# Attention, gated MLP and their gradients on one core: the first part's factors in pieces, its weights loaded inside the loop, the last gate sums in a row, and the gradients' loads moved

## The chip, the cores and the metric

The kernel runs on one core of a Trainium2 chip. A core has five engines that work side by side, each on its own list of instructions and strictly in the order of that list: TensorE (PE, matrix products; its weight loads are listed as PEld), VectorE (DVE), ScalarE (ACT), GpSimd (POOL) and SyncE (SP). Transfers between the chip's main memory and the core's two on-chip memories, SBUF and PSUM, are carried by 16 DMA engines; an engine's queue issues them. An instruction waits on semaphores until what it needs is there, and everything behind it on its engine waits with it.

The metric is the time of one execution on the device in microseconds (us). Where a time is given for a kernel, it is the median of its runs; a profile is one further execution, with a trace of every instruction.

## The reference, cut to what matters

```python
S, D, H, F = 2048, 512, 32, 1792           # Dh = 16

def _B_ref(x, w1, b1, w2, b2):
    y = _layernorm(x, axis=-1)
    h = _gelu(y @ w1 + b1)
    return h @ w2 + b2

def forward(x, wqkv, wo, w1, b1, w2, b2):
    xn = _layernorm(x, axis=-1)
    s = attention(xn, wqkv) @ wo           # 32 heads, softmax(q k / 4) v
    g = _silu(_B_ref(xn, w1, b1, w2, b2))
    return x + s * g

out, vjp = jax.vjp(forward, A_x, A_wqkv, A_wo, B_w1, B_b1, B_w2, B_b2)
return (out, *vjp(grad_out))
```

Inputs are bf16 (x and grad_out 1 x 2048 x 512). The outputs are the forward result and the gradients of x and of the six weights.

## The kernel before

The rows of x are cut into 16 tiles of 128 (`NT`), and four tiles make a group. The kernel writes its order out by hand: each engine gets its instructions in the order in which the Python code emits them, and no scheduler moves them. Nearly all transfers are issued on SP's queue (`ld = nc.sync.dma_start`, and `tr`, a transfer that transposes on its way).

There are three parts, one behind the other.

**First part** (class `Pre`, L102 to L482, up to about 220 us). At its start, x, wqkv, b1, b2, w1, the four transposed pieces of wo (`woT`, L160) and w2 are issued; POOL meanwhile clears the attention's operand 0 (`make_op`, L35, called for operand 0 at the start and for operand 1 near the end of this part): two memsets of 128 x 2048 (`KVT` L47, `QDT` L48) and two of one row (L50).

The loop over row tiles `t` (L296 to L329) works ahead of itself. In iteration t, `stats(t + 6)` takes mean and variance on DVE (L180, L181). `t_xn(t + 1)` transposes the normalised rows on PE, and DVE copies them out (`tp`, L173 to L177: four transposes into PSUM, then one copy, on DVE where its last argument is 1, on ACT where it is 0). At t = 1, 5 and 9 `factors(t + 3, t + 7)` (L183) works out the two norm factors of four tiles: a root on ACT, a reciprocal and two products on DVE, a root on ACT, a reciprocal on DVE. `norm(t + 2)` scales the rows in place on DVE (L195). `norm2(t + 2)` writes the second norm's rows on ACT (L199) into `yr`, which has four slots, so that it must wait until the store of `Y_s` (L319, two tiles, issued on SP at odd t) has read the slot. Between these, `proj3` makes the three projections (L210), and their results are copied out and transposed (`t_kvq`) for the attention. At t = 2 `bias1` turns b1 into a column (L279). Whole groups are stored at t = 4, 8 and 12 (`squares`, `stores`).

Behind the loop, from about 92.5 us, comes the hidden layer and the gate. `hid(g, fc)` is a product with w1, gelu and two stores. `gate(t)` is a product with w2, then on DVE and ACT the gate's value, the product `dsr` with grad_out (L373 to L379, called the chain) and four more operations, `gate_b` (L385 to L388), which run on POOL for t below 13 and on DVE for 13, 14 and 15. `t_ds(t)` transposes `dsr` into `dsoT`, `dproj(t)` multiplies it by `woT` (L396) and copies it to `ndc` (L397), and `t_do(t)` transposes that into `dOT`. In the loop `dproj` runs two tiles and `t_do` three tiles behind `gate`; `dsoT` and `ndc` have two slots each. The last of them, and the last `gate_b`, stand behind the loop.

**Attention** with its own gradients (`attention_core`, L1051 to L1414, about 220 to 1843 us).

**Gradients** (class `Grads`, L490 to L1048, its end from 1843 us on). A first loop over t (`emit_so`, `emit_oT`, `emit_dmT`) finishes the forward result tile by tile; `emit_dwo` (L732), from t = 12, makes the gradient of wo from `dso_all`, which is loaded in two halves (L752, L767). Then a loop over the 14 column blocks `fc` of the hidden layer: `emit_dw2(fc)` (L742) takes one transposed block `hgr` (four slots; `load_hg`, L713, a transposing transfer), and `load_hg(fc + 4)` is issued behind it. In these loops SP also issues `load_h1(a, b)` (`gp`, L659, plain loads used much later), `xn1` in four quarters (L800, L810), and `load_dkv` (`dKVn`, L790, transposing). The next loop over i makes the gradient of wqkv: `emit_dwq` from `xn1`, then `emit_dwkv` (L827) from the two halves of `dKVn`, four products each.

## Time and profile before

| | |
|---|---|
| Runs of the kernel (median, smallest, largest) | 2181.61, 2180.7, 2186.16 us |
| Profiled execution: time | 2180.46 us |
| Profiled execution: span of its trace | 2178.8 us |
| PE busy | 2133.0 us, 98% of the span |
| DVE busy | 1898.0 us, 87% |
| ACT busy | 1782.2 us, 82% |
| POOL busy | 870.6 us, 40% |
| Transfers | 461.17 MB, mean 212 GB/s |

A row of a timeline reads: start (us from the span's start), duration in us, engine, line of the kernel, operation, output <- inputs, how many follow each other; in brackets the idle time of the engine just before, and what ended it. Rows of engine SPq are SP's issues of transfers; their duration is the time that SP spent on them, not that of the transfer. A row of a line's own view begins with the line, and gives the durations in ns (smallest, median, largest) and the first and last start.

### The profile page before, as it was taken

The page shows a single profiled execution, that of the slowest core. Times are in us where ns is not written, and L with a number is a line of the kernel's source. Part 1 is how long each engine was busy: PE and PEld are TensorE (multiplying, and loading weights), DVE is VectorE, ACT ScalarE, POOL GpSimd, SP SyncE. Part 2 cuts the span into 40 slices and gives each one's busy share as a digit, 9 for nine tenths or more (in the row PEclk, how much of TensorE's full clock was granted, in tenths as well). Part 3 has the DMA queues.
Part 4 walks back from the last instruction along what each step waited for, and adds up shares of the span by engine and source line. Part 5 has one row for each costly group of instructions (what it writes and reads, how often), then busy time and mean ns, then how long its engine had stood idle before and what let it go on. Part 6 is the DMA issues. An engine that isn't in the chain of part 4 may idle for free.

```text
span 2178.8 us, 74934 instructions
## 1 busy us (share of the span) xinstructions
PE 2133.0 (98%) x30659; PEld 1170.6 (54%) x30659; DVE 1898.0 (87%) x3523; ACT 1782.2 (82%) x2481; POOL 870.6 (40%) x2397
## 2 busy tenths in 40 slices
PE   6999999999999999999999999999999999899999
PEld 3444555555555555555555555555555555444444
DVE  6677899999999999999999999999999998788647
ACT  5664899999999999999999999999999997775224
POOL 4376434343434444343434344444434343511003
PEclk9999999999999999999999999999999999999999
DMA  7786999999999999999999999999999999999975
GB/s 235 248 281 202 205 199 198 209 195 200 208 204 198 209 201 201 202 200 206 203 199 201 202 203 201 204 203 204 200 202 206 194 213 212 294 251 240 246 209 178
DMA packets 1416569, 461.17 MB, mean 212 GB/s; under 512 B 1329118, under 2 KB 1400414, under 8 KB 1416224
## 3 DMA queue, kind: packets, MB, share of 16 engines
q1 hardware_dynamic: 1401920, 425.44, 100.3%
q0 software_dynamic: 12720, 29.37, 4.9%
q8 instruction: 240, 3.93, 0.8%
q10 hardware_dynamic: 1584, 1.57, 0.2%
q14 instruction: 105, 0.86, 0.1%
HBM read 62.79 MB, written 64.75 MB: 59 GB/s over the span
## 4 chain that ended last, share of the span: by engine, by line
PE 94%; DVE 2%; DMA 1%; ACT 1%; POOL 0%; issue 0%; SPq 0%; DVEq 0%; ACTq 0%; POOLq 0%
PE tT L1192 22%; PE Z L1334 15%; PE d L1137 15%; PE X L1239 6%; PE X L1232 5%; PE X L1235 5%; PE s L1115 3%; PE ps_dy L909 2%; PE ps_dw L742 2%; PE ps_dw L983 2%; PE ps_h L352 2%; PE ps_m L367 2%; PE ps_dh L875 2%; PE tT L1266 1%; PE ps_dxa L1027 1%; PE ps_dwkv L827 1%
## 5 line engine op out<-in xcount | busy, mean ns | idle before, releaser
L1155 DVE TENSOR_TENSOR gts<-d,ets 128x512 bf16<-128x512 f32 x2048 | 1302.2, 682 | 18.2 <-PE d L1137 3.9
L1124 ACT ACTIVATE ets<-s 128x1024 bf16<-128x1024 f32 x1024 | 1051.6, 1027 | 15.2 <-PE d L1137 3.9
L1208 ACT COPY ek<-tT 128x448 f32<-128x448 f32 (+1 forms) x1024 | 525.1, 513 | 115.0 <-PE tT L1192 31.3
L1192 PE MATMUL tT<-ident_bf,ets 128*128 128x128 bf16 x6790 | 557.9, 221 | 0.0
L1192 PEld LDWEIGHTS <-ets 128*128 128x128 bf16 x6790 | 382.5, 98 | 210.5 <-issue 195.2
L1137 PE MATMUL d<-QDT,KVT 32*128 32x512 bf16 x2048 | 469.4, 384 | 0.0
L1153 POOL COPY gts<-ets 128x128 bf16<-128x128 bf16 x1024 | 281.6, 297 | 387.5 <-ACT ets L1124 382.7
L1115 PE MATMUL s<-QDT,KVT 32*128 32x512 bf16 x2048 | 401.1, 379 | 2.4 <-ACT ets L1124 2.4
L1334 PE MATMUL Z<-gk,W 128*32 128x512 bf16 x2304 | 302.9, 389 | 1.4 <-DVE acc L1348 1.3
L1239 PE MATMUL X<-gts,NAT 128*17 128x256 bf16 x4096 | 290.6, 273 | 0.0
L1232 PE MATMUL X<-ets,NAT 128*32 128x256 bf16 x4096 | 290.4, 273 | 0.0
L1235 PE MATMUL X<-ets,Lc 128*32 128x256 bf16 x4096 | 290.3, 273 | 0.0
L1334 PEld LDWEIGHTS <-W 128*32 128x32 bf16 x4096 | 105.5, 93 | 238.2 <-issue 225.0
L1137 PEld LDWEIGHTS <-KVT 32*128 32x128 bf16 x2048 | 148.5, 91 | 114.3 <-issue 21.5
L1334 PE MATMUL Z<-ek,W 128*32 128x512 bf16 x1792 | 203.6, 389 | 0.0
L1235 PEld LDWEIGHTS <-Lc 128*32 128x32 bf16 x4096 | 110.1, 97 | 108.6
L1215 DVE COPY ek<-tT 128x64 f32<-128x64 f32 x378 | 84.9, 225 | 89.5 <-ACT ek L1208 76.0
L1404 POOL COPY tick<-gts 1x2 bf16<-1x2 bf16 x205 | 36.0, 175 | 313.5 <-DVE gts L1155 313.5
L1115 PEld LDWEIGHTS <-KVT 32*128 32x128 bf16 x2048 | 142.7, 91 | 12.3 <-issue 6.4
L1239 PEld LDWEIGHTS <-NAT 128*17 128x17 bf16 x4096 | 114.7, 91 | 15.4 <-issue 1.1
L1232 PEld LDWEIGHTS <-NAT 128*32 128x32 bf16 x4096 | 108.8, 96 | 5.1 <-issue 5.1
L1295 POOL TENSOR_TENSOR W<-NATQq,rL 128x128 bf16<-128x128 bf16 x64 | 25.5, 399 | 147.9 <-DVE rL L1294 110.3
(252 smaller groups left out, 2470.4 us busy)
## 6 DMA issues: line engine op xcount, KB each, us to landing
gk<-gts SPq DMA_TRANSPOSE x512, 5.6
H1T_s<-h1r SPq DMA_DIRECT2D x28, 256.0 KB, 4.2
HGT_s<-hgT SPq DMA_DIRECT2D x8, 896.0 KB, 4.5
DH_s<-stg SPq DMA_DIRECT2D x12, 512.0 KB, 3.3
hch<-DH_s SPq DMA_DIRECT2D x12, 512.0 KB, 4.8
gp<-H1T_s SPq DMA_DIRECT2D x9, 512.0 KB, 6.8
out_dram<-ob_w POOLq DMA_DIRECT2D x36, 128.0 KB, 4.6
NAT_s<-NS SPq DMA_DIRECT2D x4, 1056.0 KB, 6.1
```

What stands on the lines that cost most here:

```text
L1115: nc.tensor.matmul(s[:, hj, :], lhsT=op["KVT"][r:r + 32, kb * 128:(kb + 1) * 128], rhs=op["QDT"][r:r + 32, qc * 512:(qc + 1) * 512], start ...
L1124: nc.scalar.activation(out=st_et[g].rearrange("k b h q -> k h b q"), in_=cur["s"][:].rearrange("k h (b q) -> k h b q", b=4), func=ACT.Exp)
L1137: nc.tensor.matmul(d[:], lhsT=op["KVT"][r:r + 32, kb * 128:(kb + 1) * 128], rhs=op["QDT"][r:r + 32, qc * 512:(qc + 1) * 512], start=True, ...
L1153: nc.gpsimd.tensor_copy(out=gts[:, kb % 2, 8, :], in_=st_et[g][:, b // 2, b % 2, :])
L1155: nc.vector.tensor_tensor(out=gts[:, kb % 2, 4 * hj:4 * hj + 4, :], in0=st_d.pop((g, hj))[:].rearrange("k (b q) -> k b q", b=4), in1=st_et ...
L1192: nc.tensor.transpose(tb[:, i - cut(g), :], et[:, b // 2, b % 2, :], ident_bf[:])
L1208: nc.scalar.copy(out=blk[j]["Ek"][kb // 4][:, kb % 4, c:7].rearrange("q i k -> q (i k)").bitcast(f32), in_=st_T[g][:, 0:(7 - c) * 64])
L1215: nc.vector.tensor_copy(out=blk[g // 16]["Ek"][kk // 4][:, kk % 4, i].bitcast(f32), in_=st_T[g][:, 448:512])
L1232: nc.tensor.matmul(X[r:r + 32, 0:256], lhsT=NATt[:, kb, hj, 1:33], rhs=ev, start=(kb == 0), stop=False, skip_group_check=True, tile_positi ...
L1235: nc.tensor.matmul(X[r:r + 32, 256:512], lhsT=Lc[:], rhs=ev, start=False, stop=False, skip_group_check=True, tile_position=(0, r))
L1239: nc.tensor.matmul(X[r:r + 17, 256:512], lhsT=NATt[:, kb, hj, 0:17], rhs=gv, start=False, stop=(kb == 15), skip_group_check=True, tile_pos ...
L1334: nc.tensor.matmul(Z[r:r + 32, :], lhsT=WT[j % 2][1 - part][:, qb, hj, :], rhs=mv, start=(part == 0 and qb == 0), stop=(part == 1 and qb = ...
```

## The change

Seven things, in the order of the diff:

1. The memset of `QDT` of operand 0 is done by DVE; that of operand 1 stays on POOL.
2. w1 (two halves, t = 3 and 5), w2 (two halves, t = 7 and 9) and the transposes of wo (two each at t = 11 and 13) are issued by a new function `weights(t)` inside the loop, behind the store of `Y_s`; before, all of them were issued ahead of the loop.
3. `factors` can be called in four parts. In the loop part 0 (first root) stays at its old place, part 1 (reciprocal and two products) follows `t_y`, part 2 (second root) follows the third projection's call `proj3(t, 2)`, and part 3 (last reciprocal) comes after the last `t_kvq`. The second root has a row of its own to write to.
4. `bias1` is called at t = 9 rather than 2.
5. At the end of the gates, the sums of gates 13, 14 and 15 follow each other on PE with only `t_ds` between them; `dproj` from 11 and `t_do` from 10 on come behind the loop, interleaved. `dsoT` and `ndc` have four slots each, the former with the help of `xnT`, which is free by then. `gate_b(13)` runs on DVE between the chains of 13 and 14; `gate_b(14)` and `gate_b(15)` come last. `t_ds(14)` is emitted twice, in the loop at t = 15 and behind it.
6. Gradients, first loop: the second half of `dso_all` is loaded at t = 3 rather than 5; five loads of `gp` come at t = 5, 7, 9, 11 and 15, where seven came at t = 3, 5, 7 and 12 to 15.
7. Gradients, loop over fc: the quarters of `xn1` are loaded at fc = 4, 6, 8 and 10, where two came ahead of the loop and two at 9 and 11; `gp` is loaded at every odd fc, where it was at the even ones from 2 on. In the loop of the gradient of wqkv, `gp`'s fourth set is loaded at i = 0 to 3, one more than before.

```diff
@@ -45,7 +45,7 @@
         t["NATQq"] = pool.tile([128, 16, 2, 16], bf16, name="NATQq")
         t["NATQd"] = pool.tile([128, 16, 2, 16], bf16, name="NATQd")
     nc.gpsimd.memset(t["KVT"][:], 0.0)
-    nc.gpsimd.memset(t["QDT"][:], 0.0)
+    (nc.vector if i == 0 else nc.gpsimd).memset(t["QDT"][:], 0.0)
     for hj in range(2):
         nc.gpsimd.memset(t["KVT"][32 * hj:32 * hj + 1, :], -1.0)
     return t
@@ -155,10 +155,17 @@
         b1_bf = sm.tile([FC, 128], bf16, name="b1_bf")
         ld(out=b1_bf[:], in_=B_b1.rearrange("(c p) -> c p", p=128))
         ld(out=b2bc[:], in_=B_b2.rearrange("(o d) -> o d", o=1).to_broadcast([128, D]))
-        ld(out=w1_sb[:], in_=B_w1.rearrange("(c p) f -> p c f", p=128))
-        for ac in range(IC):
-            nc.sync.dma_start_transpose(out=woT[:, :, ac * 128:(ac + 1) * 128], in_=A_wo[ac * 128:(ac + 1) * 128, :])
-        ld(out=w2_sb[:], in_=B_w2.rearrange("(c p) d -> p c d", p=128))
+
+        def weights(t):
+            if t in (3, 5):
+                i = (t - 3) // 2
+                ld(out=w1_sb[:, 2 * i:2 * i + 2], in_=B_w1.rearrange("(c p) f -> p c f", p=128)[:, 2 * i:2 * i + 2])
+            if t in (7, 9):
+                i = (t - 7) // 2
+                ld(out=w2_sb[:, 7 * i:7 * i + 7], in_=B_w2.rearrange("(c p) d -> p c d", p=128)[:, 7 * i:7 * i + 7])
+            if t in (11, 13):
+                for ac in (t - 11, t - 10):
+                    nc.sync.dma_start_transpose(out=woT[:, :, ac * 128:(ac + 1) * 128], in_=A_wo[ac * 128:(ac + 1) * 128, :])
 
         nc.gpsimd.memset(Bsel[:], 1.0)
         nc.gpsimd.affine_select(out=Bsel[:], in_=Bsel[:], compare_op=ALU.is_ge, fill=0.0, base=0,
@@ -180,16 +187,21 @@
             nc.vector.bn_stats(out=st6[:, t, :], in_=xt[:, t, :])
             nc.vector.bn_aggr(out=mv[:, t, :], in_=st6[:, t, :])
 
-        def factors(t0, t1):
+        def factors(t0, t1, part=None):
             r1, r2 = k.rstd1[:, t0:t1], k.rstd2[:, t0:t1]
             v = mv[:, t0:t1, 1]
             a, b = lnv[:, 0, t0:t1], lnv[:, 1, t0:t1]
-            nc.scalar.activation(out=a, in_=v, func=ACT.Sqrt, bias=k.eps_t[:], scale=1.0)
-            nc.vector.reciprocal(out=r1, in_=a)
-            nc.vector.tensor_tensor(out=b, in0=v, in1=r1, op=ALU.mult)
-            nc.vector.tensor_tensor(out=b, in0=b, in1=r1, op=ALU.mult)
-            nc.scalar.activation(out=a, in_=b, func=ACT.Sqrt, bias=k.eps_t[:], scale=1.0)
-            nc.vector.reciprocal(out=r2, in_=a)
+            c = lnv[:, 2, t0:t1]
+            if part in (0, None):
+                nc.scalar.activation(out=a, in_=v, func=ACT.Sqrt, bias=k.eps_t[:], scale=1.0)
+            if part in (1, None):
+                nc.vector.reciprocal(out=r1, in_=a)
+                nc.vector.tensor_tensor(out=b, in0=v, in1=r1, op=ALU.mult)
+                nc.vector.tensor_tensor(out=b, in0=b, in1=r1, op=ALU.mult)
+            if part in (2, None):
+                nc.scalar.activation(out=c, in_=b, func=ACT.Sqrt, bias=k.eps_t[:], scale=1.0)
+            if part in (3, None):
+                nc.vector.reciprocal(out=r2, in_=c)
 
         def norm(t):
             nc.vector.tensor_scalar(out=xt[:, t, :], in0=xt[:, t, :], scalar1=mv[:, t, 0:1], scalar2=k.rstd1[:, t:t + 1],
@@ -298,14 +310,16 @@
                 stats(t + 6)
             if t + 1 < NT:
                 t_xn(t + 1)
-            if t % 4 == 1 and t + 7 <= NT:
-                factors(t + 3, t + 7)
+            fac = (lambda part: factors(t + 3, t + 7, part)) if t % 4 == 1 and t + 7 <= NT else (lambda part: None)
+            fac(0)
             if t + 2 < NT:
                 norm(t + 2)
                 norm2(t + 2)
             proj3(t, 1)
             t_y(t)
+            fac(1)
             proj3(t, 2)
+            fac(2)
             if t >= 1:
                 t_kvq(t - 1, 1, 1)
                 t_kvq(t - 1, 2, 0)
@@ -313,11 +327,13 @@
             proj3(t, 0)
             if t >= 1:
                 t_kvq(t - 1, 0, 1)
+            fac(3)
             spread(t, 2)
             spread(t, 0)
             if t % 2 == 1:
                 ld(out=k.Y_s.rearrange("(t p) d -> p t d", p=128)[:, t - 1:t + 1], in_=yr[:, (t - 1) % 4:(t - 1) % 4 + 2, :])
-            if t == 2:
+            weights(t)
+            if t == 9:
                 bias1()
             if t % 4 == 0 and t >= 4:
                 squares(t // 4 - 1, 1)
@@ -341,8 +357,14 @@
         gd = mid.tile([128, 8, D], bf16, name="gd", tag="m4")
         gw, dsr = gd[:, 0:4, :], gd[:, 4:8, :]
         tau = mid.tile([128, D], f32, name="tau", tag="m6")
-        dsoT = mid.tile([128, 2, IC, 128], bf16, name="dsoT", tag="m5")
-        ndc = nat[:, :, 0, :]
+        dsoT2 = mid.tile([128, 2, IC, 128], bf16, name="dsoT", tag="m5")
+
+        def dsoT(t):
+            return (dsoT2, xnT)[t // 2 % 2][:, t % 2]
+
+        def ndc(t):
+            return nat[:, t % 2, t // 2 % 2, :]
+
         h1v = k.H1T_s.rearrange("(c p) s -> p c s", p=128)
         hgv = k.HGT_s.rearrange("(c p) s -> p c s", p=128)
 
@@ -377,7 +399,7 @@
                 nc.vector.tensor_scalar(out=sg, in0=ta, scalar1=0.5, scalar2=0.5, op0=ALU.mult, op1=ALU.add)
                 nc.vector.tensor_tensor(out=G_, in0=m_, in1=sg, op=ALU.mult)
                 nc.vector.tensor_tensor(out=dsr[:, t % 4, :], in0=dot, in1=G_, op=ALU.mult)
-            if t < NT - 1:
+            if t < 14:
                 chain()
             return chain, lambda e: gate_b(e, B_, G_, sg, dot)
 
@@ -388,18 +410,18 @@
             e.tensor_tensor(out=B_, in0=B_, in1=dot, op=ALU.mult)
 
         def t_ds(t):
-            tp(lambda b: dsr[:, t % 4, b * 128:(b + 1) * 128], dsoT[:, t % 2], 0)
+            tp(lambda b: dsr[:, t % 4, b * 128:(b + 1) * 128], dsoT(t), 0)
 
         def dproj(t):
             ps = psA.tile([128, 512], f32, name="ps_do", tag="mm")
             for bc in range(IC):
-                nc.tensor.matmul(ps[:], lhsT=dsoT[:, t % 2, bc, :], rhs=woT[:, bc, :], start=(bc == 0), stop=(bc == IC - 1))
-            nc.vector.tensor_copy(out=ndc[:, t % 2, :], in_=ps[:])
-            nc.gpsimd.tensor_copy(out=ND[:, (t // 4) % 2, :, t % 4, :], in_=ndc[:, t % 2, :].rearrange("p (a c) -> p a c", a=NPAIR))
+                nc.tensor.matmul(ps[:], lhsT=dsoT(t)[:, bc, :], rhs=woT[:, bc, :], start=(bc == 0), stop=(bc == IC - 1))
+            nc.vector.tensor_copy(out=ndc(t), in_=ps[:])
+            nc.gpsimd.tensor_copy(out=ND[:, (t // 4) % 2, :, t % 4, :], in_=ndc(t).rearrange("p (a c) -> p a c", a=NPAIR))
 
         def t_do(t):
             g = (t // 4) % 2
-            tp(lambda b: ndc[:, t % 2, b * 128:(b + 1) * 128], dOT[:, g, :, (t % 4) * 128:(t % 4) * 128 + 128], 0)
+            tp(lambda b: ndc(t)[:, b * 128:(b + 1) * 128], dOT[:, g, :, (t % 4) * 128:(t % 4) * 128 + 128], 0)
 
         def after(t, f=lambda: None):
             if t % 4 == 3:
@@ -423,7 +445,6 @@
         def load_dot(g):
             ld(out=dotr[:, g % 2], in_=go2[:, g * 4:g * 4 + 4])
 
-        lastb = []
         load_dot(0)
         for fc in range(FC):
             hid(0, fc)
@@ -445,22 +466,16 @@
                 gate_store(t - 1)
             if t == 0:
                 bound()
+            if t == 14:
+                continue
             chain, gb = gate(t)
             if t == 0:
                 stores_nat(3)
             if t < 13:
                 gb(nc.gpsimd)
-            else:
-                lastb.append(gb)
-            if t >= 2:
+            if t >= 2 and t < 13:
                 dproj(t - 2)
-            if t == 14:
-                lastb[0](nc.vector)
-                gate_store(13)
-            if t == NT - 1:
-                chain()
-                lastb[1](nc.vector)
-            if t >= 3:
+            if t >= 3 and t < 13:
                 t_do(t - 3)
                 after(t - 3)
             if t >= 1:
@@ -469,16 +484,32 @@
                 load_dot(g + 2)
             if 2 <= t < 6:
                 wkv_rows(t - 2)
-        t_do(NT - 3)
-        t_ds(NT - 1)
-        dso_store(NT - 1)
+            if t == 13:
+                chain14, gb14 = gate(14)
+                gb(nc.vector)
+                chain14()
+                t_ds(13)
+                gate_store(13)
 
         nc.scalar.activation(out=b2bc[0:1, 0:1], in_=b2bc[0:1, 0:1], func=ACT.Exp)
-        dproj(NT - 2)
-        dproj(NT - 1)
-        t_do(NT - 2)
-        t_do(NT - 1)
-        lastb[2](nc.vector)
+        dproj(11)
+        chain()
+        t_do(10)
+        t_ds(14)
+        dproj(12)
+        t_do(11)
+        after(11)
+        dproj(13)
+        t_ds(15)
+        dso_store(15)
+        t_do(12)
+        dproj(14)
+        t_do(13)
+        dproj(15)
+        t_do(14)
+        t_do(15)
+        gb14(nc.vector)
+        gb(nc.vector)
         after(NT - 1, lambda: gb_store(NT - 1))
 
 
@@ -761,19 +792,21 @@
                 nd += 1
             if t == 3:
                 self.load_s1(5)
-                load_h1(0, 0)
+                ld(out=dso_all[:, 8:16], in_=dsov[:, 8:16])
             if t == 5:
                 self.load_s1(6)
-                ld(out=dso_all[:, 8:16], in_=dsov[:, 8:16])
-                load_h1(0, 1)
+                load_h1(0, 0)
             if t == 7:
                 self.load_s1(7)
-                load_h1(0, 2)
+                load_h1(0, 1)
             if t in (8, 9, 10, 11):
                 load_hg(t - 8)
+            if t in (9, 11):
+                load_h1(0, (t - 5) // 2)
             if t >= 12:
                 emit_dwo(t - 12)
-                load_h1((t - 9) // 4, (t - 9) % 4)
+            if t == 15:
+                load_h1(1, 0)
         self.flush_adds()
         while nd < NT:
             emit_dmT(nd)
@@ -796,17 +829,15 @@
 
 
         nw = 0
-        for q in range(2):
-            ld(out=xn1[:, 4 * q:4 * q + 4], in_=xnv[:, 4 * q:4 * q + 4])
         for fc in range(FC):
             emit_dw2(fc)
             if fc + 4 < FC:
                 load_hg(fc + 4)
-            if fc % 2 == 0 and fc >= 2:
-                n = 7 + (fc - 2) // 2
+            if fc % 2 == 1:
+                n = 5 + fc // 2
                 load_h1(n // 4, n % 4)
-            if fc in (9, 11):
-                q = (fc - 5) // 2
+            if fc in (4, 6, 8, 10):
+                q = (fc - 4) // 2
                 ld(out=xn1[:, 4 * q:4 * q + 4], in_=xnv[:, 4 * q:4 * q + 4])
             if fc >= 11:
                 load_dkv(0, fc - 11)
@@ -843,8 +874,8 @@
                 emit_dwkv(ic, part - 1)
             if i == 0:
                 load_dkv(0, 3)
-            if i < 3:
-                load_h1(3, 1 + i)
+            if i < 4:
+                load_h1(3, i)
             if 1 <= i <= 4:
                 load_dkv(1, i - 1)
             if 4 <= i <= 10:
```

## The prediction

> **What bounds the kernel now.** I read the head of the page, then busy time by stretches, then the timeline of PE, and at each of its gaps the timeline of the engine it waits for; last SyncE's queue (SP), which issues nearly all DMAs.
>
> ```profile
> span 2178.8 us, 74934 instructions
> ...
> PE 94%; DVE 2%; DMA 1%; ACT 1%; POOL 0%; issue 0%; SPq 0%; DVEq 0%; ACTq 0%; POOLq 0%
> ...
> 9.50:92.50 83.00, 70.01 (x532) 39.17 (x531) 55.20 (x131) 50.40 (x93) 33.23 (x51) 1.00 0.72 225
> 92.50:206.00 113.50, 112.32 (x595) 53.43 (x593) 81.36 (x132) 66.38 (x102) 69.61 (x75) 1.00 0.79 260
> ```
>
> The chain of waits is 94% PE, so only PE's gaps can be won. The two window rows (length, then busy time and instructions of PE, weight loads, DVE, ACT and POOL, granted clock, DMA share, GB/s) give their place: in the loop over row tiles, 9.5 to 92.5 us, PE stands still 13.0 of 83 us; in the stage behind it 1.2 of 113.5. Time won in the loop is therefore carried on by PE. The edits touch three places: the start and loop (to 92.5), the end of the gates (206 to 220), the gradients from 1843 us on. Attention between them is not edited, and I take it as it is.
>
> **Start.** The change takes one memset of operand 0 from POOL to DVE.
>
> ```profile
> 3.41 1.80 POOL L48 MEMSET QDT<- 128x2048 bf16 x1
> 4.33 0.69 DVE L180 BATCH_NORM_STATS2 st<-xt 128x6 f32<-128x512 bf16 x1 [3.40 <-DMA xt<-in_A_x_dram]
> 5.15 3.65 POOL L50 MEMSET KVT<- 1x2048 bf16 x2
> ...
> 7.46 1.48 DVE L195 TENSOR_SCALAR xt<-xt,mv,rstd 128x512 bf16<-128x512 bf16 x1
> ...
> 9.99 1.39 DVE L195 TENSOR_SCALAR xt<-xt,mv,rstd 128x512 bf16<-128x512 bf16 x1
> 10.03 1.21 POOL L168 MEMSET NS<- 128x256 bf16 x1
> ...
> 17.11 0.40 DVE L195 TENSOR_SCALAR xt<-xt,mv,rstd 128x512 bf16<-128x512 bf16 x1
> ```
>
> The same norm takes 0.40 us at 17.11, but 1.48 at 7.46, where POOL's memsets run to 5.15 + 3.65 = 8.80 us: it ends 0.14 behind them. The next, at 9.99, ends beside the memset of 10.03 (11.24). Without 1.80 us on POOL its row ends at 7.00, so the first norm costs 0.4 and ends near 7.9 instead of 8.94. The second then meets the 10.03 memset 1.80 earlier, at 8.23 to 9.44, and ends near 9.6 instead of 11.38. I take **-1.8**; the lower bound is -1.1, the first norm's gain alone. On DVE the memset has the 3.40 us of idle time ahead of 4.33; it fits there if it takes no more than that, and the nearest row is POOL's 1.80.
>
> The Trainium skill, "SBUF — State Buffer", section "Who interferes with whom", says that a DVE tensor_scalar in a two-port mode and a GpSimd instruction exclude each other for the whole instruction. By that rule these rows are a lock and not a slowing: the trace agrees (1.48 beside 0.40, ending with the memset).
>
> **Factors in pieces.** At t = 1, 5 and 9 four rows' factors run in one go between ACT and DVE, ahead of the evacuations PE waits for.
>
> ```profile
> 19.95 0.18 DVE L188 RECIPROCAL rstd<-lnv 128x4 f32<-128x4 f32 x1 [0.71 <-ACT lnv L187]
> ...
> 22.65 0.38 PE L173 MATMUL tp_ps<-ident_bf,nat 128*128 128x128 bf16 x4 [1.42 <-DVE KT L175]
> ...
> 43.49 0.38 PE L173 MATMUL tp_ps<-ident_bf,nat 128*128 128x128 bf16 x4 [1.27 <-DVE KT L175]
> ```
>
> DVE waits 0.71 for ACT's first root, and once more for the second, with everything behind it in line; PE pays 1.42 and 1.27 at the first two passes, and I count the third as the second. The six operations stay; in pieces, one or more of the loop's four-matmul projections lie between a root and its use, so the waits are covered. If that cover fails, the 0.71 comes back at that pass. First pass: **-1.4**. At the other two a second wait stands behind:
>
> ```profile
> 19.25 3.57 SPq L319 DMA_DIRECT2D Y_s<-yr  x2
> ...
> L199 ACTq EVENT_SEMAPHORE  x1: 6467/6467/6467, 21.7 to 21.7; - x1
> ...
> L199 ACTq EVENT_SEMAPHORE  x1: 4651/4651/4651, 43.1 to 43.1; - x1
> ...
> L199 ACTq EVENT_SEMAPHORE  x1: 3535/3535/3535, 63.6 to 63.6; - x1
> ...
> 29.96 0.16 PE L279 MATMUL b_ps<-ident_bf,b_bf 14*128 14x14 bf16 x1 [2.62 <-ACT yT L177]
> ```
>
> These are ACT's waits (ns, start) at the second norm, until the store of Y_s (two row tiles) has read the buffer it writes. The waits at 43.1 and 63.6 end with stores that the group's stores at t = 4 and 8 hold up, not with the factors. A faster pass thus waits there longer; of 1.3 each I leave 0.9 and 0.7, a guess between the bounds: **-1.6** together (bounds 0 and -2.6).
>
> **Weights in the loop.** Now Y_s(0, 1) is issued at 19.25 behind four woT transposes and w2, and ACT waits 6.47 us; PE stands 2.62 us at 29.96. With the weights gone from the start, SP is free when the two rows are ready and the queue is empty: the wait goes, **-2.9** (2.62, and 0.33 at the next transpose, an estimate from the timeline there; bound -1.5, if half of the 6.47 stays). What is late next: nothing at t = 2; the transposes of t = 3 run off DVE's copies. The seven issues move to t = 3 to 13, each behind that iteration's Y_s store:
>
> ```profile
> 29.00:34.00 5.00, 3.72 (x31) 2.23 (x31) 2.61 (x7) 4.06 (x8) 2.79 (x5) 1.00 0.00 0
> ...
> 55.00:67.00 12.00, 9.81 (x79) 5.59 (x77) 8.99 (x22) 7.71 (x14) 4.32 (x6) 1.00 1.10 340
> ```
>
> A half of w1 or w2 is 0.92 MB, at 340 GB/s 2.7 us. The stretch around 31 us moves 0 GB/s and holds 5 us, room for one half or nearly two; others like it lie between the later groups' stores. The weights are read first in the stage from 92.5. In the stores' own stretches the DMA engines are full (a share of 1.10), so a late half delays the next stores. Cost 0, bound +1.0. The b1 transposes at t = 9 rather than 2: **+0.3**, their two small matmuls and copies beside full engines.
>
> First part: -1.8 - 1.4 - 2.9 - 1.6 + 0.3 = **-7.4** (bounds -5 and -8.9; not all terms fall short at once).
>
> **Last gate sums in a row.**
>
> ```profile
> 218.36 1.80 POOL L47 MEMSET KVT<- 128x2048 bf16 x1
> 219.19 0.42 DVE L388 TENSOR_TENSOR gbr<-gbr,dotr 128x512 bf16<-128x512 bf16 x1
> 219.78 1.29 DVE L1155 TENSOR_TENSOR gts<-d,ets 128x512 bf16<-128x512 f32 x2 [0.16 <-ACT ets L1124]
> ...
> 212.00:220.00 8.00, 3.88 (x31) 1.73 (x32) 7.26 (x16) 6.25 (x10) 3.42 (x4) 1.00 0.77 233
> ```
>
> PE, busy 3.88 of these 8 us, gets matmuls laid into its waits for DVE and ends some 2 us earlier, an estimate by hand. But DVE is busy 7.26 of the last 8 us, has the same operations to do (one transpose set and its ACT copy are issued once more), and attention's first DVE operation at 219.78 follows the gates' last (219.61) directly. Laid out by hand DVE ends 0.3 earlier. Against it, two more sums of DVE (tensor_scalar at their head) come to lie beside POOL's memsets of operand 1 at 218.36, and such an operation waited to the end of a memset at 7.46: +0.9 for one, +2.7 for several. I take **0**, between bounds -2.2 and +2.7.
>
> **Gradients.**
>
> ```profile
> 1872.86 1.89 PE L732 MATMUL ps_dwo<-dso_all,Oall 128*128 128x512 bf16 x8 [1.99 <-DMA dso_all<-DSO_s]
> ...
> 1888.65 13.98 PE L742 MATMUL ps_dw<-dm_all,hgr 128*128 128x512 bf16 x64
> 1908.68 16.59 PE L742 MATMUL ps_dw<-dm_all,hgr 128*128 128x512 bf16 x66 [6.06 <-DMA hgr<-HGT_s]
> ...
> 1906.30:1913.40 7.10, 4.71 (x12) 1.74 (x13) 5.61 (x8) 0.32 (x1) 0.00 (x0) 0.52 1.06 241
> ...
> 1890.46 2.27 SPq L659 DMA_DIRECT2D gp<-H1T_s  x4
> 1892.83 3.85 SPq L800 DMA_DIRECT2D xn<-XN_s  x2
> 1896.78 14.29 SPq L713 DMA_TRANSPOSE hgr<-HGT_s  x3
> 1911.79 5.86 SPq L713 DMA_TRANSPOSE hgr<-HGT_s  x2
> ...
> 1918.39 6.41 SPq L713 DMA_TRANSPOSE hgr<-HGT_s  x2
> ...
> 1938.59 5.70 SPq L790 DMA_TRANSPOSE dKVn<-dKVT_s  x1
> ...
> 1961.69 7.51 SPq L790 DMA_TRANSPOSE dKVn<-dKVT_s  x3
> ```
>
> PE waits 1.99 us for the second half of dso_all and 6.06 for the fifth block of hgr, which was issued behind four loads of gp and two of xn (1890.46 to 1896.68). Behind that wait PE's clock is 0.52 until 1913.4: 66 matmuls take 16.59, at the 64 of 1888.65's rate 14.42, so **2.2** more. All of it together: 1.99 + 6.06 + 2.17 = -10.2. The change issues dso_all at t = 3 and leaves one gp and no xn load ahead of the fifth hgr, which then leaves at about 1892.2 and lands by 1900, as PE reaches it (1888.65 + 13.98 - 1.99 = 1900.6).
>
> The loads that go from there come back behind: five more gp or xn loads among the hgr issues. SP's chain is the second bound. Its transposes take about 3.2 us each (6.41 for two), and the last of dKVn leaves at 1966.8 (1961.69 + 7.51 less its own 2.36) to land 4.7 later:
>
> ```profile
> L827 PE MATMUL ps_dwkv<-dKVn,xn x128: 379/379/379, 1959.2 to 1986.6; 128*128 128x512 bf16 x128
> ...
> DMA to landing us min/median/max: 4.7/4.7/4.7
> ...
> 1938.60:1972.00 33.40, 33.40 (x157) 15.11 (x155) 29.68 (x35) 28.87 (x28) 6.34 (x10) 1.00 1.13 258
> ```
>
> It lands at 1971.5, and PE needs it in the second half of this product, 1959.2 + 64 x 0.218 = 1973.1. The slack is 1.6 us: PE can't gain 10.2 there unless the chain gains too. Counted from 1892.2 in the new order: three hgr at 3.2 and seven, each behind a load, at 4.1 (0.5 for the load, 0.4 for the switch, an estimate from the rows above), three loads at 0.6, then the 28.2 us from 1938.59 to 1966.8 as before, and 1.2 for one load more there and its switch. The last dKVn leaves at 1892.2 + 69.5 = 1961.7 and lands at **1966.4**. So PE reaches that place 6.6 us earlier: **-6.6**, bounds -1.5 (the chain ends as now, DMA share 1.13 says it is full) and -10.2. In all, five more transposes than before stand behind a plain load. What follows is bound by PE and carries it.
>
> **Sum.** -7.4 + 0 - 6.6 = -14.0. The profiled execution took 2180.46 (span 2178.8 and 1.7 around it), 1.15 under the median of the runs (2181.61) and inside their spread: 2180.46 - 14.0 = **2166.5**.
>
> **The rivals.** *The transfers eat the gradients' gain* (chance 0.17): the DMA engines and not SP's issues set the chain, which ends as now. For it: a share of 1.11 or more throughout. Against: SP issues one transpose after another without a pause. -7.4 - 1.5 = -8.9: 2171.6.
>
> *The chain is quicker than PE* (0.07): hgr in steps of 3.0 throughout. -7.4 - 10.2 = -17.6: 2162.9.
>
> *New waits for Y_s* (0.06): the halves of w1 and w2 reach into the next group's stores and lengthen the waits of 4651 and 3535 ns by 2.7 each. For it: the full stretch from 55 us; against: idle time ahead of such stretches. -7.4 + 5.4 - 6.6 = -8.6: 2171.9.
>
> *The lock at the end of the gates* (0.04): by the full +2.7, 2169.2. The Trainium skill's rule cited above speaks for it: by that the sums would wait for each memset in full; no row of before has these sums there.
>
> *Slower* (0.08): in the stage of dw2 each hgr now stands behind a plain load, and a transpose behind loads waits until they have drained. The price is shown: the three at 1896.78 took 14.29 where two take 5.86, so the first cost 14.29 - 5.86 = 8.4, or 5.5 more than one. The loads there were six in a row; a single one has cost 0.4. With s us for each of five more such places the gradients change by -6.6 + 5(s - 0.4), and the whole is slower from s = 3.2; at s = 5.5, +11.5: 2192.
>
> **How the numbers follow.** The forecast has 0.58. Its own range is 2161.5 to 2171.5, from half of the bounds of the gates and the chain. The range for 8 times in 10 runs from -8.9 - 2.2 - 10.2 = -21.3, so about 2159, to -5 + 2.7 - 1.5 = -3.8, so 2176.7; rounded outwards, 2158 to 2177. A measurement of this kernel tells no change under 0.3%, 6.5 us, so faster means under 2175.1. From the forecast 0.55 lies below it, from the next four rivals 0.25 of 0.34, which makes 0.80 for faster; 0.13 within; 0.07 slower, nearly all of the last rival.
>
> **What would show it.** First part right: the norm at 7.5 takes 0.4; no PE wait of a us at t = 1, 5, 9; no wait of ACT near 21.7; attention starts 7 us sooner. If attention starts less than 4 us sooner, look for new ACT waits at the second norm. Gates: the last gate operation on DVE directly ahead of attention's first, no tensor_scalar over 0.5 there. Gradients right: no PE wait for dso_all or the fifth hgr, clock 1.00 around them, and a short wait for dKVn or none. Wrong: hgr issues of 5 us and more with PE waiting at each, or the dwkv product starting at the same distance from attention's end as before.

## The result, and the profile after

| | before | after |
|---|---|---|
| Median of the runs (smallest to largest) | 2180.7 us (2177.48 to 2186.16, 7 runs) | 2173.03 us (2171.67 to 2177.45, 7 runs) |
| Span of the profiled execution | 2178.8 us | 2174.8 us |
| First copy of the hidden stage (h1r, DVE) | 97.54 | 89.41 |
| Attention's first product on DVE | 219.78 | 214.28 |
| Attention's last product on DVE | 1839.91 | 1834.62 |
| First product of the stage behind dwkv (ps_dh, PE) | 1986.84 | 1981.71 |

The ratio is 0.9966 with a 95% interval of 0.9952 to 0.998: 7.7 us less by the medians, 4.4 to 10.5 by the interval, where 14.0 were forecast from the profiled execution. The profiled execution of the changed kernel was one of its slower runs (2176.54 us, 3.5 above the median). Its trace is therefore read stage by stage, each from its own start, and not by its span.

Three places, three outcomes. The first part gains 8.1 us. Of these 2.6 are gone when attention starts. From attention's last product to the stage behind dwkv the gradients take 147.1 us, against 146.9 before: nothing is left of their gain. Another 0.2 us go within attention and 1.2 behind that stage, which leaves, but for rounding, the 4.0 between the two spans.

**First part.** Rows of the changed kernel's timeline, one ACT wait from the view of line 211 (ns), and the window of the loop (columns as in the prediction):

```profile
1.11 0.91 DVE L48 MEMSET QDT<- 128x1024 uint32 x1 [0.19 <-issue]
...
7.28 0.50 DVE L207 TENSOR_SCALAR xt<-xt,mv,rstd 128x512 bf16<-128x512 bf16 x1
...
8.82 0.87 DVE L207 TENSOR_SCALAR xt<-xt,mv,rstd 128x512 bf16<-128x512 bf16 x1
...
10.48 8.70 SPq L334 DMA_DIRECT2D Y_s<-yr  x2
...
20.07 0.38 PE L180 MATMUL tp_ps<-ident_bf,nat 128*128 128x128 bf16 x4 [0.58 <-DVE KT L182]
...
36.52 0.38 PE L180 MATMUL tp_ps<-ident_bf,nat 128*128 128x128 bf16 x4 [0.49 <-DVE KT L182]
...
L211 ACTq EVENT_SEMAPHORE  x1: 6051/6051/6051, 36.2 to 36.2; - x1
...
89.41 1.41 DVE L378 TENSOR_SCALAR h1r<-ps_h,b1c 128x512 bf16<-128x512 f32 x2 [2.94 <-ACT hgT L376]
...
9.50:84.40 74.90, 70.36 (x530) 39.40 (x531) 53.43 (x130) 49.20 (x92) 31.69 (x49) 1.00 0.84 249
```

The memset on DVE takes 0.91 us, half of POOL's 1.80, in a time when DVE waited for x. The norms take 0.50 and 0.87 where they took 1.48 and 1.39. PE's waits of 1.42 and 1.27 for the copy of KT have become 0.58 and 0.49, and the wait of 2.62 is gone: the first stores of Y_s leave SP from 10.48 on, before from 19.25 on. PE stands still 4.5 of the loop's 74.9 us (before 13.0 of 83). ACT waits longer for the store of Y_s than before (6051 ns, 4651 before), but PE does not, no wait of PE there is over 0.70 us: ACT's wait has become longer and harmless.

**End of the gates.**

```profile
209.30 1.80 POOL L47 MEMSET KVT<- 128x2048 bf16 x1
...
210.47 2.52 DVE L407 TENSOR_SCALAR gbr<-gd 128x512 bf16<-128x512 bf16 x1
...
211.04 1.80 POOL L48 MEMSET QDT<- 128x2048 bf16 x1
...
214.28 2.48 DVE L1186 TENSOR_TENSOR gts<-d,ets 128x512 bf16<-128x512 f32 x4
```

The first operation of the last gate starts under one memset of POOL and ends at 212.99, behind the second (211.04 + 1.80 = 212.84), which began while it was held. It took 0.28 us before. Attention's first product waits behind it.

**Gradients.** Rows of PE and of SP's queue, the landing of the last two transfers of dKVn, and the stretch of half clock:

```profile
1882.45 38.15 PE L773 MATMUL ps_dw<-dm_all,hgr 128*128 128x512 bf16 x176
...
1929.74 3.63 PE L773 MATMUL ps_dw<-dm_all,hgr 128*128 128x512 bf16 x16 [1.30 <-DMA hgr<-HGT_s]
...
1965.01 16.87 PE L858 MATMUL ps_dwkv<-dKVn,xn 128*128 128x512 bf16 x64 [3.22 <-ACT gp3a L714]
...
1886.10 5.42 SPq L744 DMA_TRANSPOSE hgr<-HGT_s  x2
...
1923.49 3.50 SPq L744 DMA_TRANSPOSE hgr<-HGT_s  x1
...
1956.73 5.70 SPq L823 DMA_TRANSPOSE dKVn<-dKVT_s  x2
...
DMA to landing us min/median/max: 4.5/5.4/6.3
...
1964.08:1970.90 6.82, 5.89 (x14) 2.10 (x15) 3.65 (x4) 2.11 (x2) 0.00 (x0) 0.50 0.56 127
```

The wait of 6.06 us for the fifth block is gone: 176 products run without a break. SP issues the ten hgr from the fifth on, with seven loads among them, from 1886.10 to 1926.99. But PE waits 1.30 us at a late block and 3.22 us at the second half of dKVn. The view puts the latter down to an ACT operation; the last transfer of dKVn, off SP at 1962.43 and landed at 1964.9 (4.5 us after its issue at 1960.4), fits PE's start at 1965.0. From 1964.08 on the granted TensorE clock is 0.50 for 6.8 us (called half clock below), and 64 products take 16.87 us where 13.97 is the rate at full clock: 2.9 us more.

### The profile page after: what moved, and what is told of

The parts are those of the page before. It is cut to its first block, busy times and chain, and to the rows that moved or that the text cites. A ratio compares the mean times of both kernels' runs of the same rounds, so it can differ in the third digit from the quotient of the medians.

```text
span 2174.8 us, 74927 instructions
## 1 busy us (share of the span) xinstructions
PE 2135.9 (98%) x30663; PEld 1169.9 (54%) x30663; DVE 1900.2 (87%) x3524; ACT 1781.4 (82%) x2482; POOL 868.4 (40%) x2396
## 4 chain that ended last, share of the span: by engine, by line
PE 93%; DMA 3%; DVE 3%; ACT 1%; POOL 1%; issue 1%; SPq 0%; DVEq 0%; POOLq 0%; ACTq 0%
PE tT L1223 22%; PE d L1168 15%; PE Z L1365 15%; PE X L1270 6%; PE X L1263 5%; PE X L1266 5%; PE s L1146 3%; PE ps_dy L940 2%; PE ps_h L374 2%; PE ps_m L389 2%; PE ps_dw L1014 2%; PE ps_dw L773 2%; PE ps_dh L906 2%; PE ps_dwkv L858 1%; PE tT L1297 1%; PE ps_dxa L1058 1%
```

## The experiments

Twelve kernels ran. Their ratios are to the kernel before, run beside them.

**Each place by itself.** Three kernels have the change in one place only, with the code of before elsewhere.

First part alone (items 1 to 4 of the change):

> Only the first part's edits (memset on DVE, weights in the loop, factors in pieces, b1 at t = 9); the end of the gates and the gradients as before. Theory: the places add up, so the hidden stage starts 8.1 us earlier than before, as in the changed kernel's trace, attention's first DVE product about 8.1 earlier as well, and the time is about 2172.5 (before 2180.7). Rival: the end of the gates or the start of attention gives part of it back whatever their order (in the changed kernel only 5.5 of 8.2 arrive); then attention starts 5 to 6 us earlier and the time is 2175.

Measured: 2172.12 us, ratio 0.9969 (0.9957 to 0.9981). That is the whole gain of the change, 7.3 of 7.7 us. The first copy of the hidden stage comes at 89.57, 8.0 earlier, yet attention's first product only 5.65 earlier, as the rival has it. Window and PE's timeline of this run, and a window of the kernel before:

```profile
206.70:210.10 3.40, 3.08 (x11) 1.41 (x12) 2.40 (x6) 2.07 (x3) 0.00 (x0) 0.50 1.19 334
...
207.42 3.22 PE L412 MATMUL ps_do<-woT,dsoT 128*128 128x512 bf16 x8
```

```profile
220.12:226.95 6.83, 5.72 (x66) 2.52 (x61) 4.22 (x7) 4.76 (x6) 6.47 (x9) 0.50 0.95 279
```

In this execution half clock fell on the last products of the gates, which take 3.22 us where they took 1.93 before. No edit touches them. Every trace has half clock behind the gates, at attention's start, the kernel before too (its row above); in this run, and in the one with the loads on POOL's queue and the old gates, it began earlier, among the last gates (206.70 and 205.75). So no trace shows the old end of the gates behind the new first part without it.

Gates alone (item 5):

> Only the last gate sums in a row; start, loop and gradients as before. Theory (DVE's first operation of the last gate waits through POOL's two memsets of operand 1): that operation takes about 2.5 us instead of 0.28, attention's first DVE product comes 2 to 3 us later than before although PE is done 0.9 earlier, and the time is 1 to 3 us above before. Rival (the loss in the changed kernel comes from its earlier start and not from this order): no operation over 1 us there, time unchanged or 1 us less.

Measured: 2180.93 us, ratio 1.0009 (1.0001 to 1.0018), 0.2 to 4 us slower. DVE's timeline shows the lock again, though start and loop are those of before:

```profile
217.86 0.28 DVE L391 TENSOR_SCALAR gbr<-gd 128x512 bf16<-128x512 bf16 x1
...
219.73 2.52 DVE L391 TENSOR_SCALAR gbr<-gd 128x512 bf16<-128x512 bf16 x1
...
223.54 1.88 DVE L1170 TENSOR_TENSOR gts<-d,ets 128x512 bf16<-128x512 f32 x3
```

The same operation takes 0.28 ahead of the memset (218.56) and 2.52 under it. Attention's first product is 3.8 us later than before; 0.9 of that had been lost in the loop, in another stretch of half clock at 29 us.

Gradients alone (items 6 and 7):

> Only the gradients' loads moved; everything ahead as before. Theory (the transfers set the chain): PE gains 8 to 9 us up to the middle of the dw2 stage, and gives nearly all of it back at the last blocks of hgr, at the second half of dKVn (a wait of about 3 us) and in a stretch of half clock behind that wait; time within 1 us of before. Rival (the step of the prediction): 6.6 us less, 2174.

Measured: 2181.5 us, ratio 1.0008 (1.0000 to 1.0017), 0 to 4 us slower. In the trace PE is 8.4 us ahead in the middle of the dw2 stage and waits again:

```profile
1935.92 3.63 PE L742 MATMUL ps_dw<-dm_all,hgr 128*128 128x512 bf16 x16 [1.80 <-DMA hgr<-HGT_s]
1971.33 16.95 PE L827 MATMUL ps_dwkv<-dKVn,xn 128*128 128x512 bf16 x64 [4.15 <-DMA dKVn<-dKVT_s]
```

Here the wait of 4.15 us is put down to dKVn by the view itself, and 64 products take 16.95. The three ratios together make 0.9986, with some 0.0018 of uncertainty by their intervals; that overlaps the upper part of the change's own interval (0.9952 to 0.998), and whether the parts add exactly stays open.

**The lock at the end of the gates.** The calls behind the loop (`gate_b` itself is split in two for it):

```diff
-        gb14(nc.vector)
-        gb(nc.vector)
+        gb14(nc.vector, 0)      # tensor_scalar of gate 14
+        gb(nc.vector, 0)        # tensor_scalar of gate 15
+        gb14(nc.vector, 1)      # the three tensor_tensor of each
+        gb(nc.vector, 1)
```

> The changed kernel, with the first operation (tensor_scalar) of the last gates 14 and 15 emitted ahead of the other operations of both. Theory (that one operation is held by POOL's memsets): both take about 0.3 us since they start before the memset, attention's first DVE product comes 2.2 us earlier than in the changed kernel, and of that 0.5 to 2.2 are left behind the stretch of half clock; time 2171 to 2172.5. Rival (the memset holds whatever operation of DVE runs beside it): the tensor_tensor behind it takes over 1 us instead, nothing gained, 2173.

Measured: 2172.47 us, ratio 0.9971 (0.9962 to 0.9981). The timeline:

```profile
208.87 0.90 DVE L408 TENSOR_SCALAR gbr<-gd 128x512 bf16<-128x512 bf16 x2
...
209.57 1.95 POOL L47 MEMSET KVT<- 128x2048 bf16 x1
...
212.19 1.28 DVE L1191 TENSOR_TENSOR gts<-d,ets 128x512 bf16<-128x512 f32 x2
```

The same work in another order: no operation is held by a memset. The second tensor_scalar takes 0.71 beside POOL's copy of ND (209.01 to 209.62) and ends at 209.77, the memset behind it takes 1.95 instead of 1.80, the six tensor_tensor that run beside the memsets take 0.42 each, and attention's first product comes 2.1 us earlier, as the theory says. In the time of the runs this can't be seen: the ratio is that of the change within the intervals.

**The gradients' chain.** Four variants of the changed kernel, one profiled execution each, beside one of before at 2176.9 us. The table has, from attention's last product on DVE, when SP was through with dKVn and when the stage behind dwkv began on PE; the times are those of the profiled executions.

| run | SP through with dKVn | ps_dh begins | time, us |
|---|---|---|---|
| before | 129.3 | 146.9 | 2180.46 |
| changed kernel | 127.8 | 147.1 | 2176.54 |
| gradients alone | 127.2 | 147.8 | 2181.5 |
| no lock | 127.7 | 145.3 | 2170.22 |
| loads grouped | 128.2 | 145.6 | 2172.31 |
| loads on POOL's queue | 119.3 | 140.5 | 2167.21 |
| last gp later | 124.2 | 140.6 | 2168.21 |
| PE filled | 126.7 | 142.9 | 2170.55 |

Loads grouped: the plain loads of the dw2 stage, issued at every odd fc and at 4, 6, 8 and 10, are moved to three places (abridged).

```diff
-            if fc % 2 == 1: load_h1(...)           # one each
-            if fc in (4, 6, 8, 10): ld(xn1 ...)    # one each
+            for n in {3: (5, 6), 7: (7, 8, 9), 11: (10, 11)}.get(fc, ()): load_h1(n // 4, n % 4)
+            for q in {3: (0,), 7: (1, 2), 10: (3,)}.get(fc, ()): ld(xn1 quarter q)
```

> The changed kernel, with the eleven plain loads of gp and xn1 in the dw2 stage (one at a time, each between two transposing transfers) issued in three groups, at fc = 3, 7 and 10 to 11; same bytes, eight switches from load to transpose fewer. Measure: from attention's last DVE product to the first product with the second half of dKVn, 130.4 us in the changed kernel, 131.0 and 129.9 in two kernels with the same loads. Theory A (the transfers themselves fill the DMA engines): 130 to 131 still, wait of about 3 us stays. Theory B (each switch costs SP 0.4 us, the slower rival of the prediction): 127, no wait there.

Measured: eight switches fewer, and SP is through at 128.2, no sooner than with them (126.7 to 129.5 in the six other kernels with these loads on SP one by one). The 0.4 for a switch, 3.2 us for eight, is not seen: from the first of the ten hgr to the last dKVn SP needs 75.7 us here, and 75.2 to 76.3 in four kernels with single loads. Behind the larger groups transposes took longer (15.69 us for four behind three loads and 9.56 for two behind five, where four behind two took 12.40). PE waited 4.80 us at a late block of hgr, which now stood behind five loads, and so not at dKVn.

Loads on POOL's queue (abridged):

```diff
-                load_h1(n // 4, n % 4)
+                load_h1(n // 4, n % 4, nc.gpsimd.dma_start)     # likewise xn1 and gp's last four
```

> The changed kernel, with the plain loads of gp and xn1 in the dw2 stage and the loop behind it issued from POOL's queue instead of SP's; same bytes. Theory A (DMA engines full): the same distance, 130 to 131 us, from attention's last product to the second half of dKVn. Theory B (SP's issuing sets the chain: fifteen loads of 0.57 us and their switches of 0.4 leave it): 10 us or more shorter, so that PE no longer waits there (it needs about 125).

Measured: SP is through 8.5 us sooner, and PE waits under 0.6 us at any block. SP's queue, then the windows of the changed kernel and of this run:

```profile
1884.58 39.48 SPq L744 DMA_TRANSPOSE hgr<-HGT_s  x10
1924.10 27.99 SPq L823 DMA_TRANSPOSE dKVn<-dKVT_s  x8
```

```profile
1884.00:1926.00 42.00, 41.41 (x192) 18.51 (x191) 40.00 (x44) 37.55 (x33) 11.35 (x17) 1.00 1.10 269
1926.00:1956.00 30.00, 28.07 (x130) 12.35 (x129) 27.08 (x32) 23.90 (x23) 4.41 (x9) 1.00 1.12 261
```

```profile
1884.00:1926.00 42.00, 40.27 (x182) 17.74 (x185) 40.03 (x44) 36.57 (x33) 17.04 (x25) 1.00 1.10 279
1926.00:1956.00 30.00, 29.57 (x136) 13.34 (x137) 26.99 (x32) 25.25 (x24) 10.12 (x15) 1.00 1.15 293
```

In the second window 293 GB/s move where the changed kernel reached 261, with a DMA share of 1.15 and 1.12, and up to SP's last dKVn about 35 MB in both (290 GB/s over 119.3 us, 274 over 127.8). So the share over 1.1 did not mean that the DMA engines were full. The fifteen loads held SP for 8.1 us in the changed kernel, about what its chain lost. The transposes are no quicker for it: the ten hgr took 3.95 us each here, with loads beside them, and the four in 12.40 of the grouped run 3.1. What a transpose spends its time on SP with is not shown.

Last gp later: the last two loads of gp behind the last transfer of dKVn.

```diff
-            if i < 4: load_h1(3, i)
+            if i < 2: load_h1(3, i)
+            if i in (5, 6): load_h1(3, i - 3)
```

> The changed kernel, with the last two loads of gp (0.77 MB together) moved from i = 2 and 3 to i = 5 and 6, behind the last transfer of dKVn. Theory A (DMA engines full): 0.77 MB at 340 GB/s are 2.3 us, so the second half of dKVn is there 128 us after attention's last product and PE's wait of 3.2 us falls to about 1. Theory B (switches of SP): 1.9 us, nearly the same; this run tells what a repair is worth, and whether the stretch of half clock goes when the wait gets short. It would be lost again if ACT's slope operations then wait for the late loads and hold up its copies for PE.

Measured: SP is through at 124.2, 3.6 sooner, more than either theory has; given the scatter of the other kernels (126.7 to 129.5) the two are not told apart. The wait is 1.27 us, no half clock follows, and the stage behind begins 6.5 us sooner than in the changed kernel; from there to the end it is 192.0 us, 191.9 in the kernel before, so the late loads hold up nothing:

```profile
1960.67 13.99 PE L858 MATMUL ps_dwkv<-dKVn,xn 128*128 128x512 bf16 x63 [1.27 <-DMA dKVn<-dKVT_s]
```

PE filled: products whose result nobody reads, in place of the wait.

```diff
+            if i == 8:
+                ps = self.pA([128, D], f32, "ps_fill")
+                for _ in range(14):
+                    nc.tensor.matmul(ps[:], lhsT=xn1[:, 0, 0:128], rhs=dKVn[0][:, 0, :, :], start=True, stop=True)
```

> The changed kernel, with 14 products more on PE (3.1 us at full clock, their result is read by nobody) just ahead of the second half of dKVn, in place of the idle wait. Theory (PE's standing still brings the half clock): the clock stays at 1.00 there and the 64 products behind take 14.0 us instead of 16.9, so 2 to 3 us less. Rival (the half clock does not hang on that wait): the 64 products take 16 to 17 us as before, no gain.

Measured: the clock stays at 1.00 and the products behind run at full rate.

```profile
1959.06 3.19 PE L874 MATMUL ps_fill<-dKVn,xn 128*128 128x512 bf16 x14
1962.82 13.97 PE L858 MATMUL ps_dwkv<-dKVn,xn 128*128 128x512 bf16 x62 [0.58 <-issue]
...
1962.82:1976.60 13.78, 13.67 (x62) 6.27 (x65) 9.15 (x10) 9.15 (x11) 2.25 (x3) 1.00 0.64 173
```

Work that serves nothing but to keep PE busy went with full clock, and the 2.9 us are gone. This one execution doesn't show that it was the filling: the run with whole factors, below, has a wait of 3.26 us at this place and no half clock either. The section on the hardware gives what speaks for it.

**Both repairs together, and with the old gates.**

> The changed kernel with both repairs: the last gates' first operations ahead of the memset, and the gradients' plain loads on POOL's queue. From the profiles of each: attention about 2 us earlier than in the changed kernel, the second half of dKVn no longer waited for and no half clock there, 6 to 7 us from attention's last product to the end of dwkv; in all 8 us under the changed kernel, about 2164 to 2166. Rival: the two overlap with stretches of half clock that fall anew in every execution, and the median gains 4 us or less.

> As the run before it, but with the end of the gates as it was before the change. Theory (with the memset avoided the row of sums is worth 0.9 us on PE and some 2 us at attention's first product): 1 to 2.5 us slower than that run, about 2167. Rival (the order of the last gates is worth nothing, attention's start being set by DVE in both): the same time within 1 us.

Measured: 2175.43 us, ratio 0.9985 (0.9963 to 1.0007), and 2173.01 us, ratio 0.9979 (0.9957 to 1.0001). Neither beats the change, and the 1 to 2.5 us for the old gates do not show: the two intervals overlap. With the loads on POOL's queue the runs spread from 2166.5 to 2191.0 us, against 2171.7 to 2177.5 for the changed kernel (seven runs) and 2175.3 to 2187.4 for the kernel before beside them. The first run's profile is of an execution near its median (2176.51):

```profile
1883.46 45.27 SPq L749 DMA_TRANSPOSE hgr<-HGT_s  x10
...
1927.65 6.31 PE L778 MATMUL ps_dw<-dm_all,hgr 128*128 128x512 bf16 x16 [4.22 <-DMA hgr<-HGT_s]
1936.28 5.31 PE L778 MATMUL ps_dw<-dm_all,hgr 128*128 128x512 bf16 x15 [2.32 <-DMA hgr<-HGT_s]
...
hgr<-HGT_s SPq DMA_TRANSPOSE x2, 12.9
```

The ten issues that took 39.48 us take 45.27, two blocks land 12.9 us after their issue (median), and two waits and their half clock follow. SP was through with dKVn 126.6 us after attention's last product in this execution, and 120.2 in the second run's. Why two queues at once sometimes hold up the transposes wasn't settled. The repairs' expected 8 us are thus refuted as a median; 2167 is what the best executions reach.

**The first part's two levers, undone one at a time.** One execution each, 2180.96 and 2176.47 us, beside runs of before with a median of 2179.15. Weights ahead of the loop again (abridged):

```diff
+        ld(w1) ; 4 transposes of wo ; ld(w2)      # ahead of the loop, as before
         def weights(t):
+            return
```

> The changed kernel, with w1, the transposes of wo and w2 issued ahead of the loop again as before. Theory: the first store of Y_s stands behind them on SP, ACT waits about 6 us at its second norm of row tile 4, and the hidden stage starts 2.5 to 3.5 us later than in the changed kernel (87.1 to 88.1 instead of 84.57). Rival (the wait came from the factors in one go that preceded it, or SP's queue drains sooner): 0 to 1 us later.

Factors in one go again (abridged):

```diff
-            fac(0)                       # fac(1), fac(2), fac(3) later in the iteration
+            for part in range(4): fac(part)
```

> The changed kernel, with the factors in one go again at t = 1, 5 and 9 (the second root still has its own row). Theory: waits of PE of 1.3 to 1.4 us return at t = 1, 5 and 9, and the hidden stage starts 3.0 us later (1.4 and twice 0.8, the second and third partly covered by the wait for Y_s), at 87.6. Rival (once the weights are gone the stalls are hidden): under 1 us later.

First copies of the hidden stage and PE's waits, of the kernel with the weights at the start, and then of the one with whole factors:

```profile
29.43 0.38 PE L186 MATMUL tp_ps<-ident_bf,yr 128*128 128x128 bf16 x4 [3.35 <-ACT yT L190]
...
95.14 0.75 DVE L384 TENSOR_SCALAR h1r<-ps_h,b1c 128x512 bf16<-128x512 f32 x1 [2.94 <-ACT hgT L382]
...
29.80:33.20 3.40, 3.27 (x15) 1.76 (x14) 1.02 (x2) 2.71 (x6) 2.25 (x4) 0.50 0.01 2
```

```profile
20.85 0.38 PE L180 MATMUL tp_ps<-ident_bf,nat 128*128 128x128 bf16 x4 [1.36 <-DVE KT L182]
...
38.44 0.38 PE L180 MATMUL tp_ps<-ident_bf,nat 128*128 128x128 bf16 x4 [1.22 <-DVE KT L182]
...
59.13 0.38 PE L180 MATMUL tp_ps<-ident_bf,nat 128*128 128x128 bf16 x4 [1.22 <-DVE KT L182]
...
92.54 0.75 DVE L376 TENSOR_SCALAR h1r<-ps_h,b1c 128x512 bf16<-128x512 f32 x1 [2.94 <-ACT hgT L374]
```

Weights undone: 95.14 - 89.41 = 5.7 us lost, nearly twice the expected 3. PE comes to the wait earlier and so stands longer (3.35, before 2.62), and half clock follows it (0.50 at 29.8). That takes 1.7 of the 5.7: behind the wait PE is 2.10 us ahead of the kernel before (yr at 29.43, there 31.53), behind the half clock 0.44 (xt at 33.71, there 34.15). Factors undone: 92.54 - 89.41 = 3.1 lost, and the three waits are back at the size they had. Together that would be 8.8, where the two levers gain 8.1 - 1.7 = 6.4 without the memset; 1.7 of the difference is that half clock. With the weights left at the start, the factors' pieces are worth 97.54 - 95.14 - 1.7 = 0.7 us in these traces, and 2.4 without it.

## Why the prediction was right or wrong

**Start, -1.8.** Right: the first projection begins 1.7 us earlier (11.84 to 10.15), by the norms that no longer stand under the second memset.

**Factors, -1.4 and -1.6.** Right: undoing them costs 3.1 us. In the trace of the changed kernel the first pass gained 0.8 (its wait went from 1.42 to 0.58) where 1.4 was taken, the two later ones 1.3 and 0.7 where 0.9 and 0.7 were taken.

**Weights, -2.9; b1, +0.3.** Right as the lever that comes on top of the others' absence (97.54 - 92.54 - 1.7 = 3.3), somewhat small as the last one to be taken away (5.7, of which 1.7 is half clock). The b1 transposes cost nothing that shows. First part: -8.1 against -7.4.

**End of the gates, 0.** Wrong within its bounds. The prediction named the place, the rule and the price, "+0.9 for one, +2.7 for several", and gave it a chance of 0.04. Between the hidden stage and attention 2.6 us were lost in the changed kernel, 2.2 of them (2.52 - 0.28) in one operation that was held through two memsets; the order without that brought back 2.1. The step that failed is "Laid out by hand DVE ends 0.3 earlier": the layout had no lock in it. The rule of the Trainium skill ("SBUF — State Buffer", "Who interferes with whom") was the better guide here: the trace agrees with it, 2.52 us for the tensor_scalar under two memsets, 0.42 for tensor_tensor beside them, and none held by a memset when DVE came first.

**Gradients, -6.6.** Wrong, and outside its bounds of -1.5 and -10.2: +0.2 in the changed kernel, and a ratio of 1.0008 by itself. Its first half was right: the fifth block came in time, with -9.3 us up to the middle of dw2 (-14.6 there, -5.3 at attention's end). Two steps failed behind it.

The first is "So PE reaches that place 6.6 us earlier", a term of the sum that was mis-sized: PE reached the second half of dKVn 2.8 us earlier (1965.01, where 1973.1 was worked out for before, each from attention's end). SP's chain was to become 5.1 us shorter (1966.8 to 1961.7) and became 1.5 shorter (129.3 to 127.8). The ten hgr, with seven loads among them, took 40.9 us (1886.10 to 1926.99) where 38.3 were counted, and from the first dKVn to the issue of the last it was 31.6 (1928.75 to 1960.4) where 29.4 were counted. That the chain would end nearly as before is what the first rival had, but not by its cause: the same bytes came 8.5 us sooner with the loads on another queue (119.3 and 120.2, with the one execution at 126.6 against it), so the DMA engines were not what set the chain. Loads and transposes in one queue add up, and another order of the loads ahead of the last dKVn saves little; two loads taken from ahead of it saved 3.6.

The second is "What follows is bound by PE and carries it": the new wait of 3.2 us brought half clock for 6.8 us, 2.9 us more, and that took the 2.8 away. The same price had been counted at the old wait (2.2) and not at the new one.

**Other rivals.** The chain quicker than PE, with hgr in steps of 3.0, didn't come (40.9 us for ten and seven loads). New waits for Y_s came on ACT (6051 ns for 4651) and not on PE. The slower rival needs 3.2 us or more for each single load ahead of a transpose. The changed kernel itself refutes that: the transposes that stand alone behind one load take 2.85 to 4.18 us. Behind several loads the price is there (9.56 us for two in the grouped run).

**Sum.** First part -8.1, gates +2.6 and gradients +0.2 make -5.3; with 0.2 in attention and 1.2 behind that stage it is, but for rounding, the -4.0 between the two profiled spans. The medians say -7.7, with an interval from 4.4 to 10.5. The time lies inside the stated range of 2158 to 2177 and under the 2175.1 for faster, but not because the sum was right: the first part alone gives 7.3 of it, the gradients' 6.6 did not come, and an outcome with a chance of 0.04 did. The range held because it was wide enough for two rivals at once (-7.4 + 2.7 - 1.5 = -6.2), which is luck for the gradients' term.

## What to carry to other kernels

Before a load is moved along a queue, add up the queue's own time up to the next thing that PE needs from it: if only the order changes, much of a wait taken away early comes back late. Where an order is laid out by hand, lay out the neighbours' instructions too: one DVE operation of 0.28 us took 2.5 because a memset of POOL had begun first, and two lines in another order cured it. Before a lever is judged by undoing it in one execution, look for half clock: of the 5.7 us that the weights seemed worth, 1.7 was half clock behind a longer wait.
